# Attention by head pairs: all scores of a pair in one stretch, all other products of the pair before it in the next

## The chip, the core and the metric

One core of one Trainium2 chip runs the whole program, and the time is the device time of one execution in microseconds (us). The kernel before and the changed kernel are timed in turn on the same chip. The runs fell on several chips; where the times of two kernels are compared below, it is on one chip, or by ratios to the kernel before on the same chip. The profiles of before and of the changed kernel are often from different chips.

## The reference, cut to what matters

Attention over 8 batches and 8 heads of 576 tokens with 64 columns each, then a mixture of 8 experts in which a token takes the expert of its largest logit or, where its local gate is open, that of the token before it.

```python
cum = np.cumsum(np.maximum(s, 0.0), axis=-1)
scores = scale * np.matmul(q, k.transpose(0, 1, 3, 2))
scores = np.where(causal, -1e9, scores + np.minimum(-(cum[..., :, None] - cum[..., None, :]), 0.0))
attn = np.exp(scores - max);  attn = attn / (attn.sum(-1) + 1e-9)
x = np.matmul(attn, v)                       # to (B, S, H * D)
# per token: e = fresh or previous expert
out[b, s] = p[e] * (np.maximum(x[b, s] @ w1[e], 0.0) @ w2[e])
```

Of the kernel before, what the change touches and what calls it, by code (L numbers as in the profile page):

```python
# [46 lines left out]
GROUPS = ((0, 2 * P), (2 * P, S))  # L47
MIDS = (P, 13 * TL // 2)
# [3 lines left out]
    ((1, 0, P, 2 * P), (0, 0, 0, 2 * P), (NF, 1, TS, S)),  # L52
    ((0, 1, 2 * P, S), (3, 1, 3 * P, S)),
    ((1, 1, 2 * P, S),),
    ((2, 1, 2 * P, S),),
)
KEYS = [c * P for c in range(NF)] + [S - P]
# [9 lines left out]
def kernel(  # L67
# [30 lines left out]
    with ExitStack() as main:  # L98
# [40 lines left out]
        tail = attention(tc, q, k, vm, s, w_gate, w_local, ident, lg, recs, const, new_x, plan)  # L139
        tables = sort.tables()  # L140
        check = in_range(main.enter_context(tc.tile_pool(name="g_sb", bufs=1)), nc, recs, sort.total, sort.ones, out_of)
        hooks = [(0, tail), (2, last.stages[0]), (6, last.stages[1]), (11, last.stages[2]),
# [49 lines left out]
def attention(ctx, tc, q, k, vm, s, w_gate, w_local, ident, lg, recs, keep, new_x, plan):  # L192
# [24 lines left out]
    ps_s = pool("ps_s", 2, space=PSUM)  # L217
    ps_o = pool("ps_o", 1, space=PSUM)

# [12 lines left out]
    def load_v(b, p, eng=nc.sync):  # L232
        h = slice(2 * p.start, 2 * p.stop)
        for c in range(NB):
            eng.dma_start(vas[b % 2][:, c, h], vm[b][:, c, h])

# [4 lines left out]
    vas = [(once if i else p_va).tile([P, NB, H, DH], F32, name=f"va{i}") for i in range(2)]  # L241
    new_batch(0)

    load_qk(0, first, nc.scalar)
    ones = t_in.tile([BH, S], F32, name="ones")
    nc.vector.memset(ones, 1.0)
    table = once.tile([BH, 1], F32, name="table")
    nc.scalar.activation(table, ones[:, :1], Act.Exp)
    load_qk(0, slice(1, 2))
    load_v(0, first)  # L250
# [15 lines left out]
    idle = ps_o.tile([P, 512], F32, name="idle", tag="b0")  # L266

    def spin(n):
        for i in range(n):
            mm(idle[:, :P], lhsT=ident, rhs=ident, start=True, stop=True)  # L270
# [9 lines left out]
    for g, (q0, q1) in enumerate(GROUPS):  # L280
        rel = t_in.tile([BH, q1], F32, name=f"rel{g}")
        nc.vector.tensor_scalar(rel, cum[:, :q1], cum[:, MIDS[g] : MIDS[g] + 1], None, Alu.subtract)
        for c, a in enumerate(KEYS):
            if a + P <= q1:
                tr(bps[:, at : at + BH], rel[:, a : a + P], ident[:BH, :BH])
                bias_of[c, g] = at
                at += BH
    bias = once.tile([P, at], F32, name="bias")
    nc.vector.tensor_copy(bias, bps[:, :at])
    at = bias_of[NF, 1]  # L290
    nc.vector.memset(bias[: P - TL, at : at + BH], MASKED)
# [4 lines left out]
    def scores(n, u):  # L296

        b, hp = divmod(n, HP)
        qb, kb = ins[b]
        ps = ps_s.tile([P, 2, 512], F32, name="ps", tag="s")  # L300
        sc = scs[n, u] = p_sc.tile([P, 2, sum(z - a for _, _, a, z in UNITS[u])], F32, name=f"sc{u}")
        for c, g, a, z in UNITS[u]:
            at = PIECE[c, g][1]
            for h in range(2):
                d = slice(DH * h, DH * h + DH)
                mm(ps[:, h, at : at + z - a], lhsT=kb[d, hp, KEYS[c] : KEYS[c] + P], rhs=qb[d, hp, a:z],  # L306
                   start=True, stop=True)
        for c, g, a, z in UNITS[u]:
            at = PIECE[c, g][1]
            for h in range(2):  # L310
                i = bias_of[c, g] + 2 * n + h
                nc.scalar.activation(sc[:, h, at : at + z - a], ps[:, h, at : at + z - a], Act.Exp,  # L312
                                     bias=bias[:, i : i + 1], scale=scale)
        diag = [PIECE[c, g][1] for c, g, a, z in UNITS[u] if a == KEYS[c]]
        if diag:
            step = diag[1] - diag[0] if len(diag) > 1 else P
            x = sc[:, :, diag[0] : diag[0] + step * len(diag)].rearrange("p h (n c) -> p h n c", c=step)[:, :, :, :P]
            nc.gpsimd.affine_select(out=x, in_=x, compare_op=Alu.is_ge, fill=0.0, base=0,  # L318
                                    pattern=[[0, 2], [0, len(diag)], [1, P]], channel_multiplier=-1)
        if (NF, 1) in PIECE and PIECE[NF, 1][0] == u:  # L320
            at = PIECE[NF, 1][1]
            x = sc[:, :, at : at + TL]
            nc.gpsimd.affine_select(out=x, in_=x, compare_op=Alu.is_ge, fill=0.0, base=P - TL,
                                    pattern=[[0, 2], [1, TL]], channel_multiplier=-1)
# [6 lines left out]

    def add_up(n):

        add = nc.vector.tensor_tensor
        low = xs["sum", 0] = p_sm.tile([P, 2, P], F32, name="sum0")
        add(low, piece(n, 0, 0, P), piece(n, 1, 0), op=Alu.add)
        high = xs["sum", 1] = p_sm.tile([P, 2, S - 2 * P], F32, name="sum1")
        add(high, piece(n, 0, 1), piece(n, 1, 1), op=Alu.add)
        for c in (2, 3, NF):
            x = high[:, :, PIECE[c, 1][2] - 2 * P :]  # L340
            add(x, x, piece(n, c, 1), op=Alu.add)  # L341

    def values(n, g, cs):

        b, hp = divmod(n, HP)
        q0, q1 = GROUPS[g]
        if cs[0] == 0:
            xs["o", g] = ps_o.tile([P, 512], F32, name=f"o{g}", tag=f"o{g}")
        o = xs["o", g]
        for c in cs:  # L350
            a, z = PIECE[c, g][2:]
            w = piece(n, c, g)
            for h in range(2):
                mm(o[DH * h : DH * h + DH, a - q0 : z - q0], lhsT=vas[b % 2][:, c, 2 * hp + h, :], rhs=w[:, h],  # L354
                   start=(c == 0), stop=(c == (1, NF)[g]))

    def copy(n, g):
        q0, q1 = GROUPS[g]
        x = xs["t", g] = (keep if g else p_sm).tile([P, q1 - q0], F32, name=f"xT{g}")
        nc.vector.tensor_copy(x, xs["o", g][:, : q1 - q0])  # L360

    def halves(g):

        q0, q1 = GROUPS[g]
        for a in range(0, q1 - q0, TL):
            yield a // P, a, a % P

    def sums(n):

        at = S - 2 * P  # L370
        for g in range(2):
            for h in range(2):
                for t, a, p in halves(g):
                    w = piece(n, 0, 0) if g + t == 0 else xs["sum", g]
                    w = w[:, h, (a if g + t == 0 or g else a - P) :][:, :TL]
                    i = at + 2 * (2 * g + t) + h
                    for p in (p, P - TL) if 2 * g + t == NF else (p,):
                        mm(xs["o", 1][p : p + TL, i : i + 1], lhsT=w, rhs=one, start=True, stop=True)  # L378
        nc.vector.reciprocal(recs[:, n], xs["o", 1][:, at : at + 2 * NB])

    def rows(n, g, ps):
        hp = n % HP
        w = turn[:, hp].rearrange("p h w -> p (h w)")
        for t, a, p in halves(g):
            mm(ps[p : p + TL, t * 2 * HW : (t + 1) * 2 * HW], lhsT=xs["t", g][:, a : a + TL], rhs=w,  # L385
               start=True, stop=True)

    def divide(n, g, ps):

        b, hp = divmod(n, HP)  # L390
        if (b, "x") not in xs:
            xs[b, "x"] = new_x(b)
        for t0, t1, m in (((0, 2, P),), ((2, 4, P), (4, 5, TL)))[g]:
            k, i = t1 - t0, t0 - 2 * g
            x = xs[b, "x"][:m, t0:t1, 2 * hp * HW : (2 * hp + 2) * HW].rearrange("p t (h w) -> p t h w", w=HW)
            y = ps[:m, 2 * i * HW : 2 * (i + k) * HW].rearrange("p (t h w) -> p t h w", h=2, w=HW)
            rec = recs[:m, n, 2 * t0 : 2 * t1].rearrange("p (t h) -> p t h", h=2)
            nc.vector.tensor_tensor(x, y, rec.unsqueeze(3).to_broadcast([m, k, 2, HW]), op=Alu.mult)
# [14 lines left out]
    def back(n, g, ps=None):  # L413
        ps = ps_o.tile([P, 512], F32, name=f"b{g}", tag=f"b{g}") if ps is None else ps
        rows(n, g, ps)
        divide(n, g, ps)
        if g and n % HP == HP - 1:
            logits(n // HP)

    for n in range(NPAIR + 1):  # L420
        b, hp = divmod(n, HP)
        if b + 1 < B:
# [3 lines left out]
            if hp == 1:  # L426
                load_v(b + 1, slice(0, HP))
        if n < NPAIR:
            scores(n, 0)
            scores(n, 1)  # L430
        if n:
            values(n - 1, 0, (0, 1))
            values(n - 1, 1, (0, 1))
            add_up(n - 1)
            copy(n - 1, 0)
        else:
            spin(8)
        if n > 1:
            back(n - 2, 1)
        for f in plan.pop((n, 0), ()):  # L440
            f(bank)
        if n < NPAIR:
            scores(n, 2)
            scores(n, 3)
        if n:
            values(n - 1, 1, (2, 3, NF))
            sums(n - 1)
            copy(n - 1, 1)
            back(n - 1, 0)
        else:  # L450
            spin(8)
# [3 lines left out]
    return lambda bank: back(NPAIR - 1, 1, bank(1)[0])  # L455
# [786 lines left out]
```

## The kernel before: the parts that the change and the argument touch

There are 32 head pairs, 4 for each batch. TensorE makes the scores with keys on partitions, scalar takes their exps, gpsimd cuts the diagonal by selects. The values are then multiplied, the exps are added up on vector and summed over partitions by single-column matmuls against ones, and a matmul turns the result back so that tokens are on partitions and the gate's logits come along. Vector divides. Tokens are sorted by expert while attention still runs: for a group of one or two batches five stages (two with maxima and scans, then counts, rank, gates) and then one indirect scatter by gpsimd for each block of rows. A plan says after which stretch of which pair a stage is put. "Bank" is 512 fp32 columns of a pool that the kernel declares with `space=PSUM`; `ps`, `o` and `b`, which TensorE writes in the trace, lie in such pools.

```python
UNITS = (((1, 0, P, 2 * P), (0, 0, 0, 2 * P), (NF, 1, TS, S)),
         ((0, 1, 2 * P, S), (3, 1, 3 * P, S)),
         ((1, 1, 2 * P, S),), ((2, 1, 2 * P, S),))
ps_s = pool("ps_s", 2, space=PSUM)           # two score buffers, of two banks each
...
for bs in ((0, 1), (2, 3), (4,), (5,)):      # the plan of the sorting
    n0 = HP * bs[-1] + HP + 1
    g = sort.group(bs, xs)
    for f, i in zip(g.stages, (1, 3, 5, 7, 8)):
        at(n0 + i // 2, i % 2, f)
    for i, f in enumerate(g.scatters):
        i = 8 + i // 2
        at(n0 + i // 2, i % 2, f)
...
for n in range(NPAIR + 1):
    # cut: loads
    if n < NPAIR: scores(n, 0); scores(n, 1)
    if n:
        values(n - 1, 0, (0, 1)); values(n - 1, 1, (0, 1))
        add_up(n - 1); copy(n - 1, 0)
    if n > 1: back(n - 2, 1)
    for f in plan.pop((n, 0), ()): f(bank)
    if n < NPAIR: scores(n, 2); scores(n, 3)
    if n:
        values(n - 1, 1, (2, 3, NF)); sums(n - 1)
        copy(n - 1, 1); back(n - 1, 0)
    for f in plan.pop((n, 1), ()): f(bank)
```

## Time and profile before

| | |
|---|---|
| time, median of 4 | 878.76 us (877.54 to 879.72) |
| span of the profiled execution | 865.4 us |
| granted clock of TensorE, mean | 0.997 |
| TensorE busy | 847.9 us, 98% of the span |
| attention until the first expert matmul | 302.1 us |
| period of a plain pair | 8.63 us |
| sum over pairs 10 to 30 of what they last beyond 8.63 us (sorting) | 10.5 us |

Note that the profiled execution (867.0 us) took some 12 us less than the timed ones. The profile and the timing did not see the same conditions: 867 us is what three chips of the experiments give for this kernel (867.9 to 869.5), and 879 is nearer to the two others (875.7 and 876.0).

Views of the profile are read like this. In the timeline a row is: start and length of a run of instructions, engine, line, operation, what is written and from what, shapes, count and, in brackets, how long the engine had been idle ahead of it and what released it. The list of waits gives: who waited at which line, for whom, then total us, number of waits and longest one.

### The profile page before, as it was taken

To read this page: it belongs to the slowest core of one execution; us is meant where nothing else is said; L and a number is where in the kernel's file an instruction comes from. 1 tells how busy PE (TensorE), PEld (TensorE's weight loads), DVE (VectorE), ACT (ScalarE), POOL (GpSimd) and SP (SyncE) were. 2 spreads that over 40 slices of the span, in tenths; PEclk is the share of its full clock that TensorE was granted. 3 is DMA by queue.
4 is the path that set the end of the run, shared out by engine and by line. 5 is a ranking of instruction groups with operands and counts; after the bars stand their busy time and mean duration, and the time that the engine had idled before them with its cause. 6 is when DMAs were issued, how large, how long until landed. Compare 5 with 4: busy or idle time off the path is not lost.

```text
span 865.4 us, 17612 instructions
## 1 busy us (share of the span) xinstructions
PE 847.9 (98%) x7051; PEld 594.0 (69%) x7051; DVE 314.1 (36%) x837; ACT 185.5 (21%) x493; POOL 188.5 (22%) x289
## 2 busy tenths in 40 slices
PE   9999999999999999999899999999999999999996
PEld 7777677776777786586577766677657755776662
DVE  3566776678787757301111111111111111111111
ACT  5565555545555300000000000000000000000000
POOL 4322327226454205201110011000111001100001
PEclk9999999999999999999999999999999999999999
DMA  9163155833542609996599766994689935996001
GB/s 312 38 200 122 51 172 179 313 119 143 181 148 84 230 6 300 409 394 206 206 340 394 279 204 222 348 394 175 235 300 373 380 132 202 320 400 254 21 13 39
DMA packets 61403, 191.24 MB, mean 221 GB/s; under 512 B 7965, under 2 KB 9277, under 8 KB 61312
## 3 DMA queue, kind: packets, MB, share of 16 engines
q1 hardware_dynamic: 52272, 159.27, 51.9%
q0 software_dynamic: 8896, 30.47, 9.4%
q8 instruction: 57, 0.93, 0.4%
q10 hardware_dynamic: 144, 0.29, 0.1%
q14 instruction: 34, 0.28, 0.1%
HBM read 166.76 MB, written 23.76 MB: 220 GB/s over the span
## 4 chain that ended last, share of the span: by engine, by line
PE 97%; DVE 1%; issue 1%; POOL 0%; POOLq 0%; DVEq 0%
PE yp L1150 30%; PE hp L1126 28%; PE ps L306 11%; PE o L354 11%; PE b L385 5%; PE o L378 4%; PE hp L1133 4%; PE xp L1101 2%; PE idle L270 1%; DVE r_u L925 0%; DVE r_v L926 0%; PE bank L921 0%; PE bank L936 0%; PE bank L954 0%; PE bank L955 0%
## 5 line engine op out<-in xcount | busy, mean ns | idle before, releaser
L1150 PE MATMUL yp<-w,hT 128*128 128x512 f32 (+1 forms) x528 | 221.1, 594 | 0.0
L1126 PE MATMUL hp<-xT,w 128*128 128x256 f32 (+1 forms) x1088 | 193.8, 339 | 1.9 <-DVE xT L1104 1.9
L1126 PEld LDWEIGHTS hp<-xT,w 128*128 128x128 f32 x1088 | 173.2, 192 | 26.4 <-issue 7.8
L312 ACT ACTIVATE sc<-ps,bias 128x320 f32<-128x320 f32 (+4 forms) x448 | 160.4, 466 | 117.2 <-issue 56.5
L1150 PEld LDWEIGHTS yp<-w,hT 128*128 128x128 f32 (+1 forms) x528 | 88.0, 180 | 100.5 <-issue 99.5
L1157 POOL DMA_INDIRECT out_dram<-y,at x38 | 38.4, 1012 | 457.6 <-DVE y L1156 442.7
L1141 ACT ACTIVATE hT<-hp 128x512 f32<-128x512 f32 x38 | 22.7, 597 | 509.5 <-PE hp L1126 425.6
L306 PE MATMUL ps<-qk 64*128 64x320 f32 (+4 forms) x896 | 109.0, 377 | 3.1 <-DVE r_v L926 2.8
L1139 DVE TENSOR_SCALAR hT<-hp 128x512 f32<-128x512 f32 x38 | 26.2, 690 | 220.4 <-PE hp L1126 187.7
L354 PE MATMUL o<-sc,va 128*64 128x320 f32 (+4 forms) x896 | 100.8, 364 | 0.0
L318 POOL TENSOR_SCALAR_AFFINE_SELECT sc<-sc 128x256 f32<-128x256 f32 (+1 forms) x96 | 59.2, 616 | 149.2 <-ACT sc L312 101.4
L306 PEld LDWEIGHTS ps<-qk 64*128 64x128 f32 x896 | 71.6, 186 | 25.6 <-issue 5.9
L354 PEld LDWEIGHTS o<-sc,va 128*64 128x64 f32 x896 | 56.8, 136 | 42.3 <-issue 18.6
L1156 DVE TENSOR_SCALAR y<-yp,gate 128x512 f32<-128x512 f32 x38 | 28.5, 751 | 134.8 <-PE yp L1150 134.8
L341 DVE TENSOR_TENSOR sum<-sum,sc 128x640 f32<-128x640 f32 (+2 forms) x96 | 61.6, 642 | 9.8 <-POOL sc L318 4.9
L1150 PE MATMUL yp<-x,hT 128*128 128x512 f32 (+1 forms) x144 | 64.8, 595 | 0.0
L1104 DVE COPY xT<-xp 128x512 f32<-128x512 f32 x38 | 26.2, 690 | 81.2 <-PE xp L1101 81.0
L385 PE MATMUL b<-turn,xT 128*64 128x146 f32 x566 | 50.5, 291 | 0.0
L1126 PE MATMUL hp<-xT,x 128*128 128x128 f32 (+1 forms) x320 | 50.1, 317 | 0.0
L1126 PEld LDWEIGHTS hp<-xT,x 128*128 128x128 f32 x320 | 46.1, 191 | 5.8 <-issue 2.6
L990 POOL DMA_INDIRECT x_rows<-x,r_slot_i x40 | 43.3, 1083 | 11.4 <-issue 8.5
L385 PEld LDWEIGHTS b<-turn,xT 128*64 128x64 f32 x566 | 38.6, 137 | 7.8
(156 smaller groups left out, 552.9 us busy)
## 6 DMA issues: line engine op xcount, KB each, us to landing
w<-in_w_dram SPq DMA_DIRECT2D x184, 512.0 KB, 8.4
x<-in_w_dram SPq DMA_DIRECT2D x56, 512.0 KB, 9.6
qk<-in_q_dram SPq DMA_DIRECT2D x32, 288.0 KB, 4.8
va<-in_vm_dram SPq DMA_DIRECT2D x35, 256.0 KB, 4.1
qk<-in_k_dram SPq DMA_DIRECT2D x31, 288.0 KB, 5.1
xg<-x_rows POOLq DMA_DIRECT2D x30, 293.0 KB, 8.6
x_rows<-r_empty SPq DMA_DIRECT2D x6, 293.0 KB, 4.2
xg<-x_rows SPq DMA_DIRECT2D x4, 293.0 KB, 5.2
```

Of the source, the lines that this page charges most:

```text
L306: mm(ps[:, h, at : at + z - a], lhsT=kb[d, hp, KEYS[c] : KEYS[c] + P], rhs=qb[d, hp, a:z], start=True, stop=True)
L312: nc.scalar.activation(sc[:, h, at : at + z - a], ps[:, h, at : at + z - a], Act.Exp, bias=bias[:, i : i + 1], scale=scale)
L318: nc.gpsimd.affine_select(out=x, in_=x, compare_op=Alu.is_ge, fill=0.0, base=0, pattern=[[0, 2], [0, len(diag)], [1, P]], channel_multipli ...
L341: add(x, x, piece(n, c, 1), op=Alu.add)
L354: mm(o[DH * h : DH * h + DH, a - q0 : z - q0], lhsT=vas[b % 2][:, c, 2 * hp + h, :], rhs=w[:, h], start=(c == 0), stop=(c == (1, NF)[g]))
L378: mm(xs["o", 1][p : p + TL, i : i + 1], lhsT=w, rhs=one, start=True, stop=True)
L385: mm(ps[p : p + TL, t * 2 * HW : (t + 1) * 2 * HW], lhsT=xs["t", g][:, a : a + TL], rhs=w, start=True, stop=True)
L990: self.s.nc.gpsimd.indirect_dma_start(out=next(self.s.views)[:, :], out_offset=bass.IndirectOffsetOnAxis(ap=self.slot[:z, m : m + 1], axis=0),
L1126: mm(y, lhsT=w[0][:, c, f : f + P], rhs=xT[i][:, c, :], start=(c == 0), stop=(c == DK - 1))
L1133: mm(y[d, m], lhsT=w[h ^ swap][:, c, f + h * HALF : f + h * HALF + HALF], rhs=xT[i][:, c, m], start=(c == 0), stop=(c == DK - 1))
L1150: mm(ps[n * m : n * m + m, :], lhsT=hT[i][:, c, a : a + m], rhs=wn[:, c, :], start=(c == 0), stop=(c == FK - 1))
L1157: nc.gpsimd.indirect_dma_start(out=next(outs)[:, :], out_offset=bass.IndirectOffsetOnAxis(ap=at[i, k][:, 0:1], axis=0), in_=y[:, :], eleme ...
```

## The change

Its intent: the trace of before marks the scores `64*128` and the products `128*64`, and each pair goes from the one mode to the other and back twice. In that trace each way into scores and out costs 0.35 us (0.20 in, 0.15 out). The new loop goes there and back once. To that end there are three score buffers instead of two, two banks that hold the products, sums and turned rows in turn, and the 64 tail keys of both heads are stacked on 128 partitions with zero-padded weights, so that they are multiplied in the second stretch.

```diff
-    ((1, 0, P, 2 * P), (0, 0, 0, 2 * P), (NF, 1, TS, S)),
-    ((0, 1, 2 * P, S), (3, 1, 3 * P, S)),
-    ((1, 1, 2 * P, S),),
-    ((2, 1, 2 * P, S),),
+    ((0, 0, 0, 5 * TL), (3, 1, 3 * P, S)),
+    ((0, 1, 5 * TL, S), (1, 1, 5 * TL, S)),
+    ((2, 0, 2 * P, 5 * TL), (2, 1, 5 * TL, S), (1, 0, P, 5 * TL)),
 ...
-    ps_s = pool("ps_s", 2, space=PSUM)
+    ps_s = pool("ps_s", 3, space=PSUM)
+    banks = [ps_o.tile([P, 512], F32, name=f"o{g}", tag=f"o{g}") for g in range(2)]
 ...
+    def tail(n):                       # tail keys of both heads, zero-padded weights kz
+        for h in range(2):
+            mm(banks[1][DH * h : DH * h + DH, :TL], lhsT=kz[:, b % 2, hp, h], rhs=ins[b][0][:, hp, TS:], ...)
+        nc.scalar.activation(sc, banks[1][:, :TL], Act.Exp, bias=bias[:, i : i + 1], scale=scale)
 ...
+        x = xs["t", g] = p_sm.tile([P, q1 - q0], F32, name=f"xT{g}")
+        nc.vector.tensor_copy(x, banks[g][:, : q1 - q0])      # at the end of values()
 ...
     def sums(n):
+        ps = banks[0][:, SUMS : SUMS + 2 * NB]                # the sums lie in the bank of the first values
 ...
-            scores(n, 0)
-            scores(n, 1)
+        if n:
+            add_up(n - 1)
+        if n < NPAIR:
+            for u in range(len(UNITS)):
+                scores(n, u)
+        for f in plan.pop((n, 0), ()):
+            f(bank)
         if n:
-            values(n - 1, 0, (0, 1))
-            values(n - 1, 1, (0, 1))
-            add_up(n - 1)
-            copy(n - 1, 0)
-        if n > 1:
-            back(n - 2, 1)
-        for f in plan.pop((n, 0), ()):
-            f(bank)
-        if n < NPAIR:
-            scores(n, 2)
-            scores(n, 3)
-        if n:
-            values(n - 1, 1, (2, 3, NF))
-            sums(n - 1)
-            copy(n - 1, 1)
-            back(n - 1, 0)
+            values(n - 1, 0)
+            values(n - 1, 1)
+            sums(n - 1)
+            back(n - 1)
+        if n + 1 < NPAIR:
+            tail(n + 1)
         for f in plan.pop((n, 1), ()):
             f(bank)
```

Cut: loads of the tails, memsets, the biases of the tails, the bodies of `values` and `back`, the end of the loop. The plan of the sorting is unchanged.

## The prediction

> **What bounds the kernel now.** I read the page first: which engine is full, and whether the chain that ended last stays on it.
>
> ```profile
> PE 847.9 (98%) x7051; PEld 594.0 (69%) x7051; DVE 314.1 (36%) x837; ACT 185.5 (21%) x493; POOL 188.5 (22%) x289
> PEclk9999999999999999999999999999999999999999
> PE 97%; DVE 1%; issue 1%; POOL 0%; POOLq 0%; DVEq 0%
> PE yp L1150 30%; PE hp L1126 28%; PE ps L306 11%; PE o L354 11%; PE b L385 5%; PE o L378 4%; PE hp L1133 4%; PE xp L1101 2%; PE idle L270 1%; DVE r_u L925 0%; DVE r_v L926 0%; PE bank L921 0%; PE bank L936 0%; PE bank L954 0%; PE bank L955 0%
> ```
>
> TensorE is never out of work, at full clock, and 97% of the chain is its own. The expert lines (yp, hp) are about two thirds of the time and the change leaves their code alone; attention (ps = scores, o = values and sums, b = turning back to tokens) runs to about 300 us. So no wait of another engine is there to be removed; only TensorE's own time per head pair can shrink. For that I read one pair (of 32) without sorting work, in the chain in order of time (start, length, line, records):
>
> ```profile
> 58.15 1.94 PE ps L306 x20
> 60.09 1.88 PE o L354 x16
> 61.97 0.74 PE b L385 x10
> 62.71 1.28 PE ps L306 x8
> 63.99 1.13 PE o L354 x12
> 65.11 1.12 PE o L378 x39
> 66.23 0.55 PE b L385 x8
> ```
>
> Two score stretches (ps), two stretches of products (o, b). From start to start in the timeline a pair lasts 58.08 to 66.71 = 8.63 us. The next two lines (stretch, length, then busy us of PE, PEld, DVE, ACT, POOL) are that pair, and two pairs with sorting work among them:
>
> ```profile
> 58.08:66.71 8.63, 8.63 (x116) 6.28 (x115) 5.08 (x12) 5.00 (x14) 2.15 (x4) 1.00 0.05 18
> 92.67:111.74 19.07, 18.37 (x240) 13.32 (x240) 15.01 (x38) 10.27 (x29) 6.70 (x10) 1.00 0.11 35
> ```
>
> Vector has 3.5 us to spare in a plain pair, scalar 3.6. With sorting, vector rises to 7.5 us per 9.5 us: remember that.
>
> Single records inside the pair: the matmuls of two heads start 6 to 7 ns apart, so they run side by side, and each fp32 matmul is two records. Such a couple takes, start to start, 0.269 us at 320 columns, 0.216 at 256, 0.162 at 192, 0.110 at 128, 0.124 at 146, 0.056 at 64 and 0.058 at one column. Where the sum is exceeded is what matters: the last record before the second score stretch is followed after 0.218 us rather than 0.118, and the first score couple takes 0.373 rather than 0.269 (together +0.20); leaving scores, 0.366 rather than 0.269 and then 0.319 rather than 0.269 (together +0.15). So each way into scores and out costs 0.35 us, and each pair pays it twice. In the first stretch one couple after the 64-column tail piece is 0.056 late[...].
>
> [...]
>
> **The change part by part, per pair on TensorE.**
> 1. All scores in one stretch: one change of mode in and out less, −0.35.
> 2. Scores become 320+192, 256+256, 320+192 columns per head. Couples: 2×(0.269+0.162+0.216+0.216+0.269+0.162) = 2.59. Before, 128, 256, 64, 320, 192, 320, 320: 2×1.351 = 2.70. So −0.11, and the late weight load goes: −0.06.
> 3. The tail keys of both heads, stacked on 128 partitions, are multiplied by a zero-padded 64-column weight, in the mode of the products: 2×0.056 = +0.11.
> 4. Values: pieces 320, 192, 64 and 256, 256, 256, 192, 64: 2×1.353 = 2.71, as before (2.70).
> 5. Sums: 22 matmuls for 20, 11 couples for 10: +0.12.
> 6. Back: 10 for 9, but five couple slots as before: 0.
> Sum: −0.35 −0.11 −0.06 +0.11 +0.12 = about −0.29. Built from below instead: 2.59 + 2.71 + 22×0.058 + 10×0.124 + 0.11 + 0.35 + 0.03 = 8.31 us, against 8.63. I take 8.31; over 31 periods that is −9.9.
>
> Other engines: scalar gets one 64-column exp more and 64 columns per head fewer; vector one small multiply more, 1920 instead of 2048 columns to add; gpsimd four selects of 256 rather than a wide one and three. None is near 8.3. Loads: a 256 KB value chunk per batch goes, small tail loads of 256-byte rows come, all a batch ahead.
>
> **The start.** Before pair 1 the old kernel spins twice to wait for the exps of pair 0:
>
> ```profile
> 10.37 2.05 PE L270 MATMUL idle<-ident 128*128 128x128 f32 x16
> 12.35 1.35 PE L306 MATMUL ps<-qk 64*128 64x320 f32 x8
> 13.63 2.05 PE L270 MATMUL idle<-ident 128*128 128x128 f32 x16
> ```
>
> The new one spins once and has three score buffers, so pair 1's scores start about 13.7 rather than 15.61: −1.9. The new memsets on vector (about 2.1 us at the measured 1 column per ns) fit before 4.77, where it waited for the load of s.
>
> **The end.** The old kernel put the last half pair's turning back into the experts phase. Now pair 31 ends in order: with no scores to hide behind, adding up (about 2.9 us) delays the sums about 1.2 us, and the batch's logits (1.1 us on vector) stand ahead of the copy of the first expert rows. The first expert matmul came 9.4 us after the last score work; I work out 10.5: +1.1.
>
> **Sorting stages.** All but the last of each group stand at the end of a pair, on vector ahead of the next adding up. The stage with the scans occupies vector 2.9 us:
>
> ```profile
> 101.87 0.68 DVE L925 TENSOR_SCALAR r_u<-bank 2x512 f32<-2x512 f32 x1
> 102.47 0.67 DVE L926 TENSOR_SCALAR r_v<-bank 2x512 f32<-2x512 f32 x1
> 103.44 1.35 DVE L928 TENSOR_TENSOR_SCAN r_v<-r_u,r_v 2x576 f32<-2x576 f32 x1
> PE ps L306 <- DVE r_v L926: 2.8, 4, 0.7
> ```
>
> The last line, of the list of waits, is what it cost before: 0.7 us, four times, because the stage sat in one of two score buffers. With three that goes. In its place: sums now come 5.5 us after the scores begin, and need the adding up (2.9) and the first copy (0.4) behind the stage on vector; I get about 0.9 us late there and 0.25 in the stage with the maxima. 1.1 − 0.7 = 0.4 each, four groups: +1.6.
>
> **Sum.** −9.9 −1.9 +1.1 +1.6 = −9.1. From 878.93: 869.8; I say 869.5, since about 0.05 us of the old pair that I could not place may go too.
>
> **Rivals.**
> - The second stretch becomes a chain that TensorE waits in. Two banks hold values, sums and rows in turn. The turning back into the first bank must wait for the reciprocal that reads it: the last sum starts, 0.20 us later it is read, the reciprocal lasts 0.22, TensorE may go on at +0.48; the two couples in the other bank fill until +0.53. The next tail needs the division of the other bank: that ends at 1.21 (0.75 + 0.46), TensorE needs it at 1.27. Both fit by 0.05 us only. For it: so little slack. Against: read-to-start delays are the measured 50 to 60 ns. If both miss by 0.1 us, 32 pairs give back 6.4 us: 876.
> - Vector sets the pair. 5.1 us of work in 8.3 with the path division, adding up, copy at 4.5 us against 5.5: no in plain pairs; in sorting ones yes, and if each of five stages stalled 1 us, 20 us in four groups would go: 885. Against: rank and gates are 2.2 and 1.7 us, inside the slack of about 1.5 us plus their own matmuls.
> - A change of mode costs little[...]. Then only −0.29 + 0.35 remains and, with the ends and the sorting, the time is near 881. Against: the starts are late by the same 0.20 and 0.15 at every switch.
> - More is won: old sorting pairs cost 9.6 us over the plain period in all. If the third buffer removed a third of that, 866.
>
> **Range and chances.** The slot sum is firm to 0.05 us per pair (1.6 us), stalls add up to 5, the ends ±2. Range 864.5 to 875.5. Faster by over 2% needs under 861.3, 17.6 us, a pair of 8.06 us at the same ends: that is 0.04. Slower by over 2% needs stalls of 0.8 us in each pair: 0.02. Within 2%: 0.94.
>
> **What would show it.** A plain pair in the chain of waits: one score stretch of 12 couples near 2.8 us including its switches, no piece of ps between two of products, period 8.25 to 8.4. Waits of TensorE on vector under 0.1 us before the turning back and before the tail in plain pairs; near 0.9 us before sums in scan stages only. Pair 1's scores near 13.7, first expert matmul near 292 to 293 rather than 302. From there to the end 563 us, as before. A plain period of 8.6 would mean that the switch was no cost; waits before the tail would make the tight chain the cause.

The sum: −9.9 −1.9 +1.1 +1.6 = −9.1, from 878.93 to 869.8, said as 869.5. The "late weight load" of point 2 is the couple that came 0.056 us late in the trace of before; that a weight load delays it was the author's reading and is not shown.

## The result, and the profile after

The changed kernel took 917.14 us, median of 4 (912.66 to 921.91), the kernel before 878.76 beside it. The ratio is 1.0438, with an interval of 1.0382 to 1.0495: slower by over 4%, where a gain of 1% was predicted. (A ratio is the mean time of one kernel's fast runs over that of the other's of the same rounds, so it is not quite the ratio of the medians quoted.)

The page of the changed kernel:

```profile
PE 864.3 (95%) x7359; PEld 622.0 (68%) x7359; DVE 316.8 (35%) x841; ACT 189.0 (21%) x525; POOL 178.1 (20%) x295
PEclk9999888998988899999999999999999999999999
PE 89%; DVE 7%; issue 2%; another core or an unknown queue 1%; POOL 0%; POOLq 0%; SPq 0%; DVEq 0%
```

The clock row shows the surprise first: from the fifth slice on (91 us and later) the granted clock drops again and again, all within attention. And vector now holds 7% of the chain that ended last, where it held 1%.

Where is the loss? Not in the plain pair. This is one, in the chain in order of time, as the prediction showed one of before:

```profile
80.22 2.79 PE ps L340 x24
83.01 2.87 PE o L395 x32
85.88 0.88 PE o L419 x31
86.76 0.12 PE o L414 x4
86.88 0.23 PE o L419 x8
87.11 1.32 PE o L432 x20
88.43 0.02 issue
```

One score stretch, one of products, no wait in between. The windows view gives its length, and that of one pair with sorting in it (after the length come the busy times of TensorE, its weight loads, vector, scalar and gpsimd, and then the clock):

```profile
80.15:88.49 8.34, 8.34 (x129) 6.76 (x125) 6.17 (x16) 5.11 (x15) 2.07 (x4) 1.00 0.64 195
119.98:134.69 14.71, 10.11 (x126) 7.40 (x125) 8.73 (x29) 4.79 (x14) 6.11 (x10) 0.88 0.54 179
```

A plain pair lasts 8.34 us in all of them, as predicted. The sorting pair lasts 14.71. Added up over the pairs from the first sorting stage on, what lies beyond 8.34 us is 62.9 us, where it was 10.5 in the profile of before. (That profile is probably from a chip of another kind. On chip 7, where both kernels were traced later, it is 70.2 against 15.0.) The loss is there. Three things make up most of it, and all three are in that one pair, in the timeline (cut):

```profile
119.98 3.18 PE L340 MATMUL ps<-qk 64*128 64x320 f32 x24
120.33 0.41 DVE L446 TENSOR_REDUCE lg<-pair 128x36 f32<-128x144 f32 x1
...
122.28 0.45 DVE L991 TENSOR_TENSOR r_rank<-r_rank,r_hot 128x80 f32<-128x80 f32 x1
...
124.93 1.37 DVE L379 TENSOR_TENSOR sum<-sum,sc 128x512 f32<-128x512 f32 x2
...
125.74 0.28 PE L395 MATMUL o<-tail,vz 128*64 128x64 f32 x4
...
127.36 0.17 DVE L1008 TENSOR_TENSOR r_idp<-r_idp,r_den 128x10 f32<-128x10 f32 x1
127.44 0.81 DVE L398 COPY xT<-o 128x320 f32<-128x320 f32 x2
...
127.98 0.40 PE L419 MATMUL o<-one,sc 128*64 128x1 f32 x8 [1.96 <-DVE xT L398]
...
129.05 0.38 PE L419 MATMUL o<-one,sum 128*64 128x1 f32 x8
...
132.31 0.22 DVE L420 RECIPROCAL recs<-o 128x10 f32<-128x10 f32 x1 [4.05 <-remote]
132.58 1.73 PE L432 MATMUL o<-turn,xT 128*64 128x146 f32 x12 [2.60 <-issue]
```

**First, a wait for vector.** TensorE is done with the values at 126.02 and starts the sums at 127.98. The sums go into the bank of the first values, and the trace has them wait 1.96 us until vector has copied the values out (`<-DVE xT L398`). That the shared bank is the reason is shown by own_bank below; this order is called the guard of the bank. Vector has the logits (L446), the rank (L991), the adding up (L379) and the gates (L1008) to do before that copy, all in one pair: it starts 7.5 us into the pair, and vector was busy for 6.9 of them.

**Second, a late signal.** The last sum starts at 129.23. The reciprocal that reads the sums starts 3.07 us later, with vector idle for 4.05 us. In a pair without sorting it starts 0.24 us after the last sum. TensorE waits as well: the next rows go into the bank that the reciprocal reads, and it goes on at 132.58, 0.05 us after the reciprocal ends. (The profile puts this wait down to nothing, "issue"; in three other pairs it names the reciprocal.)

**Third, the clock.** The same score stretch at full clock and after such a wait:

```profile
88.49 2.86 PE L340 MATMUL ps<-qk 64*128 64x320 f32 x24
108.18 5.49 PE L340 MATMUL ps<-qk 64*128 64x320 f32 x24
```

The clock records have 54.6 us at half clock in attention; the kernel before had none there, and its first 3.4 us at 303 us, as the experts begin. The list of waits sizes the first two. The first line is the wait for vector; the next is how long vector stood idle for the late signals, and the last two are what TensorE itself lost behind them:

```profile
PE o L419 <- DVE xT L398: 12.2, 10, 2.0
DVE recs L420 <- remote: 22.6, 6, 4.3
PE o L432 <- issue: 7.2, 3, 2.6
PE o L432 <- DVE recs L420: 6.3, 3, 2.4
```

From the first expert matmul, 345.53 us, to the end it is 565.5 us, where it was 563.3: the experts are not the cause.

### The profile page after: what moved, and what is told of

It is laid out like the page before. It is cut to its first block, busy times and chain, and to the rows that moved or that the text cites. A ratio compares the mean times of both kernels' runs of the same rounds, so it can differ in the third digit from the quotient of the medians.

```text
span 911.1 us, 18343 instructions
## 1 busy us (share of the span) xinstructions
PE 864.3 (95%) x7359; PEld 622.0 (68%) x7359; DVE 316.8 (35%) x841; ACT 189.0 (21%) x525; POOL 178.1 (20%) x295
## 4 chain that ended last, share of the span: by engine, by line
PE 89%; DVE 7%; issue 2%; another core or an unknown queue 1%; POOL 0%; POOLq 0%; SPq 0%; DVEq 0%
PE yp L1177 29%; PE hp L1153 26%; PE ps L340 9%; PE o L395 7%; PE o L432 5%; PE o L419 4%; PE hp L1160 4%; PE xp L1128 2%; DVE sum L379 2%; DVE sum L376 1%; PE o L294 1%; PE o L363 1%; DVE xT L398 1%; DVE r_v L955 0%
## 5 line engine op out<-in xcount | busy, mean ns | idle before, releaser
L346 ACT ACTIVATE sc<-ps,bias 128x256 f32<-128x256 f32 (+3 forms) x448 | 153.8, 481 | 35.5 <-PE ps L340 35.2
L350 POOL TENSOR_SCALAR_AFFINE_SELECT sc<-sc 128x256 f32<-128x256 f32 x128 | 67.9, 536 | 210.7 <-ACT sc L346 203.2
L340 PE MATMUL ps<-qk 64*128 64x320 f32 (+2 forms) x768 | 103.4, 418 | 2.1 <-DVE r_v L953 2.0
L395 PE MATMUL o<-sc,va 128*64 128x256 f32 (+3 forms) x896 | 91.4, 355 | 0.8 <-DVE tail L373 0.8
L340 PEld LDWEIGHTS ps<-qk 64*128 64x128 f32 x768 | 76.4, 206 | 21.3 <-issue 6.2
L432 PE MATMUL o<-turn,xT 128*64 128x146 f32 x640 | 54.6, 318 | 13.6 <-issue 7.2
L432 PEld LDWEIGHTS o<-turn,xT 128*64 128x64 f32 x640 | 41.5, 150 | 17.6 <-issue 8.4
L379 DVE TENSOR_TENSOR sum<-sum,sc 128x128 f32<-128x128 f32 (+2 forms) x96 | 52.3, 545 | 3.3
L436 DVE TENSOR_TENSOR x<-o,recs 128x292 f32<-128x292 f32 x64 | 34.4, 538 | 27.1 <-PE o L432 20.5
```

What stands on the lines that cost most here:

```text
L340: mm(ps[:, h, at : at + z - a], lhsT=kb[d, hp, c * P : c * P + P], rhs=qb[d, hp, a:z], start=True, stop=True)
L346: nc.scalar.activation(sc[:, h, at : at + z - a], ps[:, h, at : at + z - a], Act.Exp, bias=bias[:, i : i + 1], scale=scale)
L350: nc.gpsimd.affine_select(out=x, in_=x, compare_op=Alu.is_ge, fill=0.0, base=0, pattern=[[0, 2], [1, P]], channel_multiplier=-1)
L379: add(y, y, piece(n, c, g), op=Alu.add)
L395: mm(banks[g][DH * h : DH * h + DH, a - q0 : z - q0], lhsT=v, rhs=w, start=(i == 0), stop=(i == len(some) - 1))
L432: mm(ps[p : p + TL, t - t0], lhsT=xs["t", g][:, at : at + TL], rhs=w, start=True, stop=True)
```

## The experiments

The expectations name theories by letters: A is that the new order itself is faster, as predicted, and B its rival; C is that the late signals come from the scatters of gpsimd; E is that the halved clock is a loss of its own on top of the waits; J is that the guard of the bank in which the sums lie, and not vector's work as such, holds TensorE up. Other letters are rivals of these.

Times of all timed runs, with the ratio to the kernel before on the same chip (two looks at the kernel before stand in the text):

| run | chip | us | before there | ratio |
|---|---|---|---|---|
| changed, first measurement | not told | 917.14 | 878.76 | 1.0438 |
| after_late | 4 | 922.75 | 869.23 | 1.0609 |
| before_late | 4 | 933.91 | 869.23 | 1.0735 |
| scatter_first | 4 | 884.98 | 869.23 | 1.0170 |
| fill | 4 | 889.85 | 869.23 | 1.0243 |
| after_again | 1 | 883.80 | 869.45 | 1.0168 |
| fill_sums | 1 | 872.58 | 869.45 | 1.0033 |
| copies_act | 1 | 862.85 | 869.45 | 0.9912 |
| copies_act_moved | 1 | 863.25 | 869.45 | 0.9927 |
| after_third | 6 | 883.84 | 867.92 | 1.0185 |
| copies_act_again | 6 | 862.27 | 867.92 | 0.9931 |
| own_bank | 6 | 867.95 | 867.92 | 1.0003 |
| after_fourth | 10 | 920.41 | 875.74 | 1.0512 |
| scatter_inside | 10 | 909.97 | 875.74 | 1.0393 |
| own_bank_act | 10 | 870.99 | 875.74 | 0.9944 |
| after_fifth | 7 | 919.43 | 875.97 | 1.0481 |
| no_scatter | 7 | 889.48 | 875.97 | 1.0172 |

### Is the new order itself faster? (after_late, before_late)

In both kernels all sorting of the first four groups goes behind the attention loop. The result is wrong, since rows are overwritten by then; the loop is what is looked at.

```diff
-            for f, i in zip(g.stages, (1, 3, 5, 7, 8)):
-                at(n0 + i // 2, i % 2, f)
-            for i, f in enumerate(g.scatters):
-                ...
+            for f in (*g.stages, *g.scatters):
+                at(NPAIR, 1, f)
```

> The changed kernel with all four sorting groups moved behind the attention loop (wrong output on purpose: four of the eight x buffers are overwritten before they are scattered; same work otherwise). If the loss lies only where sorting stages meet the one-stretch order (theory A), all 31 pair periods are 8.34 us, the clock stays at 1.0 in the loop, pair 32 begins near 272 us, and this kernel is about 9 to 11 us faster than the old kernel with the same move. If the new order loses by itself (rival B: bank guarding, clock, loads), periods above 8.34 appear here too.

> The old kernel with the same move, as the partner. Theory A: pair periods of 8.63 us throughout, last pair done about 9.6 us earlier than in the old kernel (its measured excess in sorting pairs), and the time 9 to 11 us above the changed kernel with the same move. Rival B: below or equal to it.

922.75 against 933.91 us: the new order is 11.2 us faster between medians (10.2 between means) when no sorting lies in it, where the prediction had −9.9 − 1.9 + 1.1 = −10.7. The four times of the one (922.4 to 925.3) and of the other (930.0 to 936.2) do not overlap. In the two traces the last pair's scores begin 8.8 us earlier: 0.7 of it at the start and 8.1 in the pairs. From pair 1 on all periods are 8.34 us in the one; in the other they are 8.63, but for pair 1 with 7.95. The clock is full throughout the loop:

```profile
PEclk9999999999996556999999999999999999999999
```

(The drop, half clock from 283 to 361 us, is the sorting alone, with TensorE mostly idle.) So A is shown: the change does what it should, and the loss comes from its meeting with the sorting.

### Do the scatters make the signals late? First try (scatter_first)

```diff
-                i = 8 + i // 2
-                at(n0 + i // 2, i % 2, f)
+                at(n0 + 4 + i // 4, 1, f)
```

> The changed kernel with the scatters of a group issued only at the end of a pair, four at a time, ahead of the next pair's selects on gpsimd, so that they run beside scores and values and no longer beside sums. If the late completion of the sums (2.3 to 3.3 us in six pairs, about 16 us in all) comes from scatters running beside the sums (theory C), reciprocals start 0.24 us after the last sum everywhere and the time falls 15 to 30 us, clock included, to 888 to 902. If four scatters in a burst do it wherever they stand (rival D), something else is late by 2 to 3 us and the time stays within 8 us of 917.

884.98 us, ratio 1.0170, with no late signal at all. It looked like a triumph and was a mistake: the order of instructions turned out to be the same as in the changed kernel, on gpsimd and on every other engine that matters. I had repeated the changed kernel on another chip. What it showed is that chips differ: on this one there is no late signal, and the loss is 15 us instead of 38.

### Is the halved clock a loss of its own? (fill, after_again, fill_sums)

The test of E: TensorE gets dummy matmuls to do while it waits. If E holds, the clock stays up and the waits alone remain.

```diff
+    def fill(k):
+        t = bank(1)[0]
+        for _ in range(k):
+            mm(t[:, :P], lhsT=ident, rhs=ident, start=True, stop=True)
 ...
+            fill(FILL_SUMS.get(n))     # sorting pairs only
             sums(n - 1)
```

> The changed kernel with dummy matmuls of 0.22 us each put where TensorE waited (before the sums and before the second turning back, somewhat fewer than the measured wait), so that it is never idle. If the halved clock (54.6 us at half speed in the trace) is the second half of the loss (theory E), the clock stays near 1.0 and the time falls 15 to 27 us, to 890 to 902. If the clock is a mere companion (rival F), the time stays within 6 us of 917 or rises.

889.85 us, 4.9 us slower than the unfilled kernel on that chip (scatter_first stands for it), though the clock in attention was full. I had sized the dummies by the first trace, with a second set for the late signals before the second turning back. On this chip those waits do not exist, so the dummies became waits themselves. Inconclusive, by my own sizing. The next had the same edit with dummies before the sums alone, 3 to 7 of them as the undisturbed waits ask, and the unaltered kernel beside it.

> The changed kernel, not altered. The run named scatter_first turned out to have the very same order of instructions on gpsimd, scalar, vector and TensorE as the changed kernel, and it took 885 us where the changed kernel had taken 917 on another chip. If the late completions of the sums belong to that chip or to those runs and not to the program, this run gives 880 to 890 on a chip where the old kernel takes 869, with reciprocals 0.24 us after the last sum. If the position of the scatters mattered after all, it gives 905 or more.

> The changed kernel with dummy matmuls only before the sums of the eight pairs in which TensorE was seen to wait there for vector (1.0 us, and 1.6 to 2.0 us), three to seven of 0.22 us each, a little less than the wait. The waits on vector stay (13 us in all), only the idleness goes. Theory E (the halved clock that follows the wait is a loss of its own, 27 us at half speed in the attention part of scatter_first): no half clock before the experts and 9 to 14 us less than after_again. Rival F (the clock is a companion): within 3 us of after_again.

883.80 and 872.58: 11.2 us come from the clock alone. The waits before the sums in after_again, in the list of waits:

```profile
PE o L419 <- DVE xT L398: 13.2, 11, 2.0
```

The pair of above, first in after_again:

```profile
126.01 0.40 PE L419 MATMUL o<-one,sc 128*64 128x1 f32 x8 [1.96 <-DVE xT L398]
127.67 2.69 PE L432 MATMUL o<-turn,xT 128*64 128x146 f32 x20
127.86 0.22 DVE L420 RECIPROCAL recs<-o 128x10 f32<-128x10 f32 x1 [1.58 <-PE o L419]
```

and in fill_sums:

```profile
123.30 1.83 PE L459 MATMUL bank<-ident 128*128 128x128 f32 x14
125.33 0.40 PE L419 MATMUL o<-one,sc 128*64 128x1 f32 x8 [0.20 <-DVE xT L398]
126.63 1.44 PE L432 MATMUL o<-turn,xT 128*64 128x146 f32 x20
```

The wait for vector is as long, only filled; the turning back takes 1.44 us rather than 2.69. Half clock in attention falls from 24 us to none; the next 6.8 us of it come from 305.4 us on, where the experts begin. E is shown. And the reciprocal of after_again is 0.29 us after the last sum: no late signal here.

When does the clock halve? The records change it in steps of 3.41 us (in the first trace of the changed kernel every stretch of half clock in attention lasts 3.41 or 6.83 us), and I laid that grid, whose steps are the windows below, over the idle time of TensorE in after_again and no_scatter. All eight windows with 1.89 to 2.10 us of idle were followed by one at half clock. Of the eight with 1.02 to 1.71 us four were: the ones that held 50 to 60 starts of matmuls beside the idle time, and not those that held 18 to 36. None with 0.87 us or less was. So 1.02 to 2.10 us of idle time in one window were followed by half clock in 12 of 16 cases. In the first trace, up to the first expert matmul, it was all five windows with 1.93 to 2.08 us, four of six with 0.90 to 1.73 us (those with 50 to 64 starts, not those with 17 and 28), and one of 73 with less (0.79 us). The same count over all 20 traces (the windows at full clock ahead of the experts) bears this out: of 42 windows with 1.75 us or more of idle, 41 were followed by half clock. Of 59 with 0.9 to 1.75 us it was all 33 that held 40 starts or more, and 2 of the 26 with fewer. Below 0.9 us it was 3 of 1565 (0.55 to 0.79 us), so the edge is not sharp. Why the lower clock went with more starts was not shown.

### Is it the copy that holds the sums? (copies_act, copies_act_moved)

The copies out of the banks go to scalar, which has 3 us to spare in each pair; the third unit's exps are put behind the first copy.

```diff
-        nc.vector.tensor_copy(x, banks[g][:, : q1 - q0])
+        nc.scalar.copy(x, banks[g][:, : q1 - q0])
 ...
+            exps[0](); exps[1]()
             values(n - 1, 0)
+            exps[2]()
             values(n - 1, 1)
```

> The changed kernel with the two copies of the value products out of their banks done by scalar rather than vector (the first between the exps of the second and third score unit). Theory G (the sums wait because everything that vector has to do for a pair, the sorting stages included, stands in line before the sums): vector loses 0.85 us of the line, the waits before the sums fall from 1.0 to about 0.5 and from 1.95 to about 1.0 us, 13 us to 6 in all, the clock halves less, and the time falls 8 to 15 us below after_again. Rival H (the sums wait for the bank, so a copy by any engine comes as late): the waits stay within 0.2 us of what they were and the time within 4 us.

862.85 us, 21 us less than the changed kernel and less than the kernel before. The same pair:

```profile
120.79 0.43 ACT L403 COPY xT<-o 128x320 f32<-128x320 f32 x1
122.27 0.35 PE L424 MATMUL o<-one,sc 128*64 128x1 f32 x8
122.54 0.23 DVE L1012 TENSOR_REDUCE r_den<-r_ex 128x10 f32<-128x80 f32 x1
123.79 0.22 DVE L425 RECIPROCAL recs<-o 128x10 f32<-128x10 f32 x1
```

The first copy ends at 121.22, the sums start 1 us later with no wait, and the gates run beside them. What is left of TensorE's waits before the sums in the whole kernel is two of at most 0.3 us. A plain pair lasts 8.39 us here rather than 8.34, some 1.7 us over 30 pairs; why was not looked for.

The second kernel also moves the stages to later places, `(2, 4, 5, 8, 9)`, and the scatters with them, so that rank and gates do not fall in one pair.

> As copies_act, and the four heavy sorting stages moved so that vector does them after the adding up (choose, rows and rank at the middle of a pair) and no two of them fall in one pair. Theory G: no wait of TensorE on vector above 0.3 us, the clock at 1.0 through attention, the gain of the plain pairs comes through: 8 to 13 us faster than the old kernel. If other waits appear, the time lies between that of copies_act and the old kernel.

863.25 us, no better: waits of 0.4 to 0.6 us came back at other places. This other plan had nothing left to save; my expectation of more was wrong.

### Or the bank? (after_third, copies_act_again, own_bank)

The sums go into a bank of their own, and the copies stay on vector:

```diff
-        ps = banks[0][:, SUMS : SUMS + 2 * NB]
+        ps = bank(1)[0][:, : 2 * NB]
```

> The changed kernel once more, in the hope of the kind of chip on which it took 917 us (there the old kernel took 879). Theory I (late completions are a matter of that chip): if the old kernel takes about 879 here, six or so reciprocals are 2 to 3 us late and this run is near 917; if the old kernel takes about 869, none is late and this run is 881 to 887.

> The changed kernel with the copies on scalar, again. 6 to 9 us faster than the old kernel on the same chip where nothing completes late; where completions are late, it shows whether they also come without waits before the sums: within 2% of the old kernel if not, 15 us or more above it if so.

> The changed kernel with the row sums written to a bank of the score pool, so that they no longer wait until vector has copied the value products out of the first bank; the copies stay on vector. If the guarded bank is what holds the sums (theory J), the waits before the sums fall to under 0.5 us; the turning back, 1.3 us later, must still wait for the copies behind the stages, so a part comes back there: waits of 12.7 us in all become 3 to 7 and the time is 5 to 11 us below the unaltered changed kernel. If the adding up itself is what comes late (rival K), the waits stay before the sums and the time within 3 us.

867.95 us against 883.84: 15.9 us less, more than I expected. The waits before the sums on the copy are gone, though vector does the same work in the same order; a smaller wait takes their place one step later, where the turning back needs the copied values themselves:

```profile
PE o L432 <- DVE xT L398: 3.9, 4, 1.1
```

So J is shown: what held TensorE was the guard of a bank that sums and values share, and the clock followed (mean granted clock of the profiled execution 0.989, against 0.979 in after_third). copies_act_again gave 862.27 beside it, the better of the two mends, and repeated its first result.

> The old kernel, for a trace from the same chip: pairs of 8.63 us, first expert matmul near 302 us; if this chip takes 879, it shows where the 10 us above 869 lie.

A look at the kernel before gave 868.80, with a trace like the first: TensorE waits four times for 0.7 us and once for 0.4 behind sorting stages, and there is no half clock in attention.

### The late signals (after_fourth, scatter_inside, own_bank_act, after_fifth, no_scatter, before_third)

The fourth call happened on a chip of the other kind, as the first line of it shows.

```diff
 scatter_inside
-                i = 8 + i // 2
-                at(n0 + i // 2, i % 2, f)
+                at(n0 + 5 + i // 4, 2, f)       # between the selects of the first and the third unit
```

> The changed kernel. 881 to 887 us with no late reciprocal on a chip where the old kernel takes about 869; near 917 with late ones where it takes about 879.

> The changed kernel with the scatters between the selects of the first and third score unit, up to four in a pair and a pair later, so that they run beside scores and values. On a chip with late completions, theory C (scatters beside sums cause them) wants no late reciprocal and 25 us or more less than after_fourth; otherwise the same as there. On a chip without them: within 4 us of after_fourth, as the waits before the sums stay.

> Both cures at once: the sums in a bank of the score pool and the copies on scalar. As either alone removes the wait at the sums, and the copies on scalar also the one at the turning back, there is little left: 859 to 865 us where the old kernel takes 869, within 3 us of copies_act.

920.41, 909.97 and 870.99 us. scatter_inside gained 10 us and not the 25 that C asked for. But C has a finer test inside that run. Of the ten pairs with scatters, the gpsimd was among its scatters at the last sum in four, and there the reciprocal came 1.60 to 2.33 us after it; in the six others its last scatter had ended about 1 us earlier or more, and the reciprocal came after 0.23 to 0.29. And between the sums TensorE itself now stopped in short gaps that are put down to nothing (issue):

```profile
138.79 0.33 PE L418 MATMUL o<-one,sum 128*64 128x1 f32 x5 [0.45 <-issue]
139.19 0.97 POOL L1019 DMA_INDIRECT x_rows<-x,r_slot_i  x1 [0.30 <-issue]
139.51 0.23 PE L418 MATMUL o<-one,sum 128*64 128x1 f32 x2 [0.40 <-issue]
140.97 1.79 PE L431 MATMUL o<-turn,xT 128*64 128x146 f32 x13 [0.96 <-issue]
141.25 0.22 DVE L419 RECIPROCAL recs<-o 128x10 f32<-128x10 f32 x1 [3.43 <-PE o L418]
```

TensorE goes on in bursts at 138.06, 138.79, 139.51 and 140.97. The records of semaphores have the completions of the scatters in bursts at 138.01 to 138.16, 139.47 to 139.60 and 140.93 to 140.99: the same moments for three of the four; none is on record near 138.79.

own_bank_act is own_bank and copies_act in one. On this chip its reciprocals still come 1.05 to 1.17 us late in four pairs, but all that TensorE still waits for behind them is the division, 2.5 us in four waits, and it is 49 us faster than the changed kernel and, at 0.9944 (0.991 to 0.9978), faster than the kernel before.

The last takes the scatters away. The rows are filled by plain transfers in pairs 4 to 11 instead, so that what is read later is defined; the result is wrong (its error is nan).

```diff
-            for i, f in enumerate(g.scatters):
-                i = 8 + i // 2
-                at(n0 + i // 2, i % 2, f)
+        for i in range(48):
+            at(4 + i // 6, i // 3 % 2, lambda bank, e=i // 6, c=i % 6: nc.sync.dma_start(
+                next(sort.views)[e * R + c * P : e * R + c * P + P, :], sort.empty))
```

> The changed kernel once more, as the yardstick of this chip. Two kinds of chip were seen: on three of them the ratio to the kernel before was 1.017 to 1.0185 and no reciprocal came late, on two it was 1.044 and 1.051, with six reciprocals or more that came 2.3 to 4.9 us after the last sum. On a chip of the first kind: 883 to 886 us. On one of the second kind: 912 to 926.

> The changed kernel without the scatters of the first four groups (wrong result on purpose; the rows are filled with empty rows by plain transfers in pairs 4 to 11 instead, so that all that is read is defined). Theory C (late completions come from a scatter in flight): no reciprocal comes more than 0.35 us after the last sum, on either kind of chip; on a chip of the second kind that takes 25 us or more off the changed kernel, on one of the first kind within 4 us of it. Rival (late completions belong to the chip and to the waits of TensorE, the scatters only lie beside them): on a chip of the second kind late reciprocals stay in pairs 13, 14, 21, 25. The waits on vector before the sums, about 13 us, stay in both theories, as vector's work is the same.

> The kernel before, with a profile on this chip. On a chip of the second kind, theory C expects its own reciprocals or other signals to come late beside scatters too, by about 1 us each, as it took 6 to 9 us more there than on the three others; on one of the first kind, a trace like that of the prediction, 866 to 869 us.

The call fell on a chip of the second kind, and it settles C there: 919.43 against 889.48 us, 30 us less. The ratio of 1.0172 is that of the chips without late signals, partly by chance: in the traces the first expert matmul comes 38.9 us earlier (314.6 against 353.6), but the experts last 572.1 us against 566.7, which was not looked into. The pair of above:

```profile
126.62 0.40 PE L419 MATMUL o<-one,sc 128*64 128x1 f32 x8 [1.95 <-DVE xT L398]
127.69 0.52 PE L419 MATMUL o<-one,sum 128*64 128x1 f32 x8
128.25 0.22 DVE L420 RECIPROCAL recs<-o 128x10 f32<-128x10 f32 x1 [1.35 <-PE o L419]
```

The wait for vector is there, the late signal is not. No reciprocal of the run is late. In after_fifth the row of the waits had been

```profile
DVE recs L420 <- remote: 26.1, 6, 5.3
```

before_third, 875.26 us, shows that the kernel before has late signals on this chip too, in four pairs, but small ones, 0.1 to 0.7 us more than on the first trace: its scatters have mostly ended when its last sum comes, or begin after it. The kernel before is slower on chips 7 and 10 by 6 to 8 us. In this single look four pairs of the scatters (15, 23, 24 and 27) last 4.5 us more than on the first trace, with TensorE's own short stops and 3.4 us of half clock among them, and the experts take 567.6 us against 563.3; more was not looked for.

A scatter beside the sums is not enough by itself: in after_again, on chip 1, one was running at the last sum in nine pairs, and the reciprocal came after 0.24 to 0.29 us in all of them.

## Why the prediction was wrong, point by point

- **The pair: right.** 8.31 us predicted, 8.34 measured, in every plain pair of every run of the changed kernel; the first of the two sums, −0.29, was exact. The terms for the change of mode (−0.35), for the scores and for the sums hold as a sum; the switch that is left still costs 0.35 us in the trace, around the score stretch at 80.15 (0.20 in, 0.15 out). Multiplying by 31 was too much: the kernel before did its pair 1 in 7.95 us, so from pair 1 to pair 31 it is 8.1 us (before_late and after_late) and not 9.9.
- **The start: right in kind, smaller in size.** Pair 1's scores at 13.45 us (about 13.7 said) in the first trace, but at 13.98 to 14.67 in four later ones. Beside the kernel before on one chip it is 0.7 us earlier (chips 4 and 7) to 1.3 (chip 6), not 1.9.
- **The end: right in size.** The first expert matmul comes 10.6 us after the last pair's start plus one plain period (10.5 said). By the same count it is 9.1 in the kernel before, not 9.4, so the end cost 1.5 us and not 1.1. The experts' own part was 2.2 us longer than in the profile of before.
- **The rivals: the second one happened.** "Vector sets the pair", in sorting pairs and not in plain ones, is what the runs show, and its reason against, that rank and gates fit in the slack, is what failed. That its 885 us is near the 883.8 of chips 1 and 6 is luck: it has 20 us of stalls, where there are 13 us of waits and 11 of clock. The tight chain fitted in plain pairs, without a wait, and the change of mode was a cost (0.35 us), as a plain period of 8.6 would have denied; it is 8.34. For "more is won", the excess of old sorting pairs is 10.5 us by pairs 10 to 30, not 9.6, and it grew.
- **"Sorting stages": the step that failed.** It gave 1.1 us to a scan stage, called rank and gates "inside the slack", and came to +1.6. On the undisturbed chips what the sorting pairs last beyond the plain period is 33.6 us (after_again) against 10.5 (in both the first trace of before and before_again): +23.1. Two terms were wrong.
  - The waits: 13.2 us at the sums on chip 1, in 11 waits, against about 4.6 in my working (four groups at 0.9 + 0.25). The waits that it named came as said: 1.0 us in the scan pairs 11, 19 and 23 and 0.26 in pairs 10 and 18. What it did not have is 1.6 to 2.0 us in pairs 13, 21, 25 and 29, with rank and gates, and 2.0 in pair 27, where another stage of sorting stands behind the scan. I had set rank (2.2 us) and gates (1.7) each against 1.5 us of slack and its own matmuls. But the plan puts the rank at the end of one pair and the gates in the middle of the next, and vector meets both in the same pair, ahead of the same copy, with a batch's logits in some. Together they make up to 2 us of wait.
  - The clock: 11.2 us, with no term in the sum at all. I took the clock as a given of the kernel before.

  Of the +23.1, the waits are 9.8 (12.9 in these pairs against 3.1 before) and the clock 11.2; some 2 us remain unplaced. The whole sum can be taken on chip 6, where both kernels were traced (after_third and the single look before_again): start −1.3, plain pairs −8.1, sorting +24.6, end +1.2 counted from the last pair's start, experts −2.1. That is +14.4 before rounding, the difference of the two spans.
- **A third term, on some chips.** 30 us more on chip 7 (919.43 against 889.48) from signals that come late while scatters are in flight, part of it again by way of the clock (0.962 in the profiled execution, against 0.980 without the scatters). On the chip of the first measurement that was most of the loss: its sorting excess of 62.9 us compares with 33.6 on chip 1 and, on chip 7, with 70.2 with the scatters and 31.8 without them.
- **The starting point** was a timed 878.93 us, while the profile that the working reads is of an execution of 867.0; the prediction does not ask why.
- **The range** was built from "stalls add up to 5". It held the arithmetic of TensorE and left out that a wait of 1 to 2 us had a price of nearly its own size again (11.2 us by the clock for 13.2 us of waits on chip 1).

What stays open is how TensorE's signals, and in one run its instructions, come to be late while a scatter is in flight, and why only on some chips. Shown is that on chip 7 vector stood idle 26.1 us in six waits for late signals with the scatters, and that without them no reciprocal was late; which part of a scatter, its instruction or its transfers, was not told apart. Open too is whether the first measurement was on a chip of that kind or on the very one.

## What to carry to other kernels

When a stretch is merged, ask for every buffer that is guarded as a whole which engine frees it and what that engine does first, and add up all the work that a plan puts ahead of it in the worst stretch, not each piece against the slack. Here the bank that held two things made the second wait for the reader of the first, 12.2 us in the first trace and 13.2 on chip 1: giving the sums a bank of their own took 16 us, handing the copy to an engine with time to spare took 21. And a wait of TensorE of 1 to 2 us cost about twice its length here, as the clock followed it down (13.2 us of waits, 11.2 more by the clock).
